# Second shifted copy in two halves, each on VectorE or GpSimd, in a newly planned order

## The chip, the cores and the metric

The kernel runs on one core of a Trainium2 chip. The time is device microseconds (us) of one execution. Three executions of the kernel before took 707.72, 704.95 and 707.62 us, so its median is 707.62 us.

## The reference, cut to what matters

Two attention blocks read the same input x (2048 tokens, 512 features, 32 heads of 16), and a gate per token mixes them. Block B is the expensive one: full softmax attention, 32 heads of 2048 x 2048 scores.

```python
def _A_ref(x, wqkv, w_phi, wo):
    ...
    pq = jnp.einsum("bhsd,hdf->bhsf", q, w_phi)
    pk = jnp.einsum("bhsd,hdf->bhsf", k, w_phi)
    phi_q = jnp.concatenate([_softmax(pq, axis=-1), _softmax(-pq, axis=-1)], axis=-1)
    phi_k = jnp.concatenate([_softmax(pk, axis=-1), _softmax(-pk, axis=-1)], axis=-1)
    kv = jnp.einsum("bhsf,bhsd->bhfd", phi_k, v)
    ...
    num = jnp.einsum("bhqf,bhfd->bhqd", phi_q, kv)
    den = jnp.einsum("bhqf,bhf->bhq", phi_q, z)[..., None] + 1e-6
    ...

def _B_ref(x, wqkv, wo):
    ...
    scores = jnp.einsum("bhqd,bhkd->bhqk", q, k) * (Dh ** -0.5)
    p = _softmax(scores, axis=-1)
    o = jnp.einsum("bhqk,bhkd->bhqd", p, v)
    return (lambda x, *d: x.transpose(*d))(o, 0, 2, 1, 3).reshape(B, S, D) @ wo

x = A_x
g = _sigmoid((x * gate_w).sum(-1, keepdims=True))
a = _A_ref(x, A_wqkv, A_w_phi, A_wo)
b = _B_ref(x, B_wqkv, B_wo)
return g * a + (1 - g) * b
```

## The kernel before, in words

**Sets and tiles of block B.** The work of block B is cut into 32 sets (`N_SETS`): four chunks of 512 queries, in each four groups of eight heads, in each two sets of four heads. A set runs over 16 key tiles of 128 keys. For one key tile TensorE multiplies keys by queries for four heads: four score products (`qk`, line 1231), each 128 x 512 into one bank of the PSUM tensor `psR`, which has seven banks. The exponential of the scores comes from one of two engines:

- ScalarE takes two banks at a time and writes a tile `E` (line 1246, a 128 x 1024 exponential), so two instructions make a key tile. There are 12 buffers for `E`.
- VectorE makes a cheap exponential: it scales a bank of scores into the bits of a bfloat16 number and writes them as int16 into a tile `T` (line 1251, 128 x 512, four instructions for a key tile). To make this exact enough, two shifted copies of `T` are made, `TS` = `T` + 43 and `TS` = `T` + 85 in integers. The products with the values then use three weighted terms. The first copy is always VectorE's (line 1263, one instruction over 128 x 2048). The second (`m >= PSH`) is either the same on VectorE or, on GpSimd, an addition of int32 numbers that hold two int16 each (line 1266, 128 x 1024 int32).

Then TensorE multiplies with the values (`pv`, line 1282, four matmuls of 18 columns side by side) into the one bank `psO`: one round for an `E` key tile, three rounds for a `T` key tile. At the end of a set VectorE copies `psO` into `OT` (line 866), a transposing DMA and two VectorE instructions (lines 1172, 1174) normalise it, and the next set's first `pv` has to wait for that copy of `psO`.

**The rest.** In the first sets also run: the projections of keys, queries and values of all groups (lines 883 and 945, evacuated mostly by VectorE), the gate (line 988: 64 matmuls with one column each, in four parts; then an exponential on ScalarE, line 992, and `omg`, lines 993 to 995), the product of block A's projection with `w_phi` (line 1006, 128 x 128 matmuls, evacuated by VectorE into `Wp`) and a check of magnitudes (sums of squares by matmuls with `ones`, line 1023, maxima on VectorE into `ct`). From set 4 on block A runs in between: projections, exponentials on ScalarE (line 1074), sums and normalisation on GpSimd (lines 1080 to 1090), from set 13 on also the second half of block A (`nums`, line 1150) and the output products (line 1326).

**What sets the order.** Nothing of the order is written by hand. When the kernel is built, a list scheduler (`_Sched`) places every operation with a planned cost (`occ`), a priority and the buffers that are free, and issues the operations of each engine in that planned order. Waits on semaphores are derived from the plan. Whether a key tile goes to ScalarE or VectorE, and whether the second copy goes to VectorE or GpSimd, is chosen in the plan too: both forms are offered as alternatives (`alt`), and the first that the plan can place wins (`choose`). The tuple `STYLES` holds one number for every 3 us of the plan. It seeds the thresholds by which the scheduler weighs score products against other work in that stretch, so another tuple is another order.

The plan keeps VectorE's copies (`kind="sh"`) and GpSimd's work apart in time: a GpSimd operation gets a dependency on the latest VectorE copy planned before it, and a VectorE copy is planned behind the GpSimd work that has been placed (`port`, in `_earliest` and `advance`).

After planning, `fill` looks for stretches of 3.413 us in which the planned work of TensorE is under a share (`CELLS`) of full use of its array, and puts idle matmuls (products with zeros into `psO`, line 1379) into gaps there. In that sum a gate part counts 0 and `nums` counts 1.

Of the kernel before, what the change touches and what calls it, by code (L numbers as in the profile page):

```python
# [38 lines left out]
GT = 2.2  # L39
# [27 lines left out]
Q32, PSH, SHP = 1, 2, 1.88  # L67
# [5 lines left out]
HAM, CELLS = 3.413, 0.46  # L73
# [35 lines left out]
class _Sched:  # L109
# [58 lines left out]
    def _place(self, o, at):  # L168
# [21 lines left out]
        for slots, ts in single.items():  # L190
            times = self._slot_times(slots)
            if len(times) < len(ts):
                return None, None
            got = sorted(times, key=lambda i: (max(times[i], when), -i))[:len(ts)]
            when = max([when] + [times[i] for i in got])
            where += list(zip(ts, sorted(got)))
# [191 lines left out]
    def fill(self, make, narrow, last_pv, set_O):  # L388
# [10 lines left out]
        for i, o in enumerate(pe):  # L399
# [3 lines left out]
                0.0 if o.name in ("gate", "gsum") else 1.0)  # L403
# [310 lines left out]
def _build(ctx, nc, A_x, A_wqkv, A_w_phi, A_wo, B_wqkv, B_wo, gate_w, out):  # L714
# [76 lines left out]
    def st_(x):  # L791
        return T0 + P_SET * x
# [190 lines left out]
    for part in range(4):  # L983
# [7 lines left out]
        gops.append(add("pe", st_(GT), 0.9, gate_mm, deps=sum(op_x, []) + op_gw, tiles=[tg], mode="full", name="gate", nb=st_(GT - 0.7)))  # L991
# [211 lines left out]
    for s in range(N_SETS):  # L1203
# [12 lines left out]
        for eng, frac, kt in todo:  # L1216
# [40 lines left out]
            else:  # L1257
                di = DSET.index(kt)
                sh = []
                for m, X in ((1, T1), (2, T2)):  # L1260
                    two = m >= PSH
                    a2 = lambda eng: alt + ((("sh", s, kt, m), eng),) if two else alt
                    sh.append([add("dve", pr + 1.0 + 0.3 * m, 0.6, lambda e, T=T, X=X, m=m: e.tensor_single_scalar(  # L1263
                        X.ap, T.ap, SHIFT[m], ALU.add), deps=exps, tiles=[T, X], name="sh", kind="sh", alt=a2("dve"))])
                    if two:
                        sh[-1].append(pool(pr + 1.0 + 0.3 * m, SHP, lambda e, T=T, X=X, m=m: e.tensor_tensor(  # L1266
# [194 lines left out]
```

## Time and profile before

| | |
|---|---|
| median of three runs | 707.62 us (704.95 to 707.72) |
| profiled execution, its own time | 709.42 us |
| its span (first to last instruction) | 707.6 us |
| mean granted TensorE clock | 0.99 of full speed |
| exponentials on ScalarE (line 1246) | 692, i.e. 346 key tiles |
| scaled scores on VectorE (line 1251) | 664, i.e. 166 key tiles |
| copies on VectorE (line 1263) | 205: 166 first and 39 second ones |
| second copies on GpSimd (line 1266) | 127 |

The span is 1.8 us shorter than the time of the same execution. Busy time is the time in which an engine had at least one instruction running. Consecutive instructions of ScalarE or VectorE overlap at their ends, so a run of n instructions takes less than n times the mean of one. The lines of the profile stand in the prediction, where they are used.

### The profile page before, as it was taken

How to read it: one execution, taken by the hardware profiler on the slowest of the kernel's cores; microseconds unless marked ns; L12 is line 12 of the kernel's file. 1: busy time of each engine (PE TensorE's matmuls, PEld its weight loads, DVE VectorE, ACT ScalarE, POOL GpSimd, SP SyncE). 2: the span in 40 equal slices, each digit the busy share in tenths (PEclk: the TensorE clock that was granted, in tenths of full speed). 3: DMA queues.
4: the chain of work that ended last, by engine and by line, in shares of the span. 5: the costliest groups of instructions: out<-in, count | busy, mean ns of one | idle time of the engine just before them, and what ended most of it. 6: DMA issues, size and time to landing. Idle time of an engine off the chain costs nothing.

```text
span 707.6 us, 16129 instructions
## 1 busy us (share of the span) xinstructions
PE 657.1 (93%) x6632; PEld 208.6 (29%) x6632; DVE 667.4 (94%) x1191; ACT 679.7 (96%) x769; POOL 429.3 (61%) x364
## 2 busy tenths in 40 slices
PE   8999999999999999989999999999999999988895
PEld 3333343332322222222222322222222222222222
DVE  5998899999999999999999999999999999999995
ACT  6999799999999999999999999999999999999994
POOL 5468666655756656656667766666666755566541
PEclk9999899999999999999999999999999999999998
DMA  6501000011000000102111121112212111220001
GB/s 145 154 16 10 13 12 16 17 59 25 10 16 16 9 17 8 24 8 36 34 31 38 46 54 28 40 40 45 38 31 47 42 32 35 38 45 9 16 9 34
DMA packets 72192, 23.80 MB, mean 34 GB/s; under 512 B 64048, under 2 KB 72112, under 8 KB 72112
## 3 DMA queue, kind: packets, MB, share of 16 engines
q1 hardware_dynamic: 70896, 21.93, 14.7%
q8 instruction: 53, 0.87, 0.6%
q10 hardware_dynamic: 1216, 0.79, 0.4%
q14 instruction: 27, 0.22, 0.1%
HBM read 4.21 MB, written 2.10 MB: 9 GB/s over the span
## 4 chain that ended last, share of the span: by engine, by line
ACT 77%; PE 15%; DVE 5%; DMA 1%; issue 0%
ACT E L1246 73%; PE psR L1231 5%; PE psO L1282 4%; PE psR L883 3%; DVE T L1251 3%; ACT phk L1074 2%; ACT WAT L1074 2%; PE psR L1326 1%; PE psR L945 1%; DMA OTT<-OT 1%; DVE TS L1263 1%; PE psR L897 1%; PE psR L1023 0%; DVE vB L950 0%; PE psR L1006 0%
## 5 line engine op out<-in xcount | busy, mean ns | idle before, releaser
L1246 ACT ACTIVATE E<-psR 128x1024 bf16<-128x1024 f32 x692 | 649.1, 1118 | 12.0 <-PE psR L1231 10.9
L1251 DVE TENSOR_SCALAR T<-psR 128x512 int16<-128x512 f32 x664 | 424.1, 678 | 19.9 <-PE psR L1231 16.5
L1231 PE MATMUL psR<-qz,kT 32*128 32x512 bf16 (+1 forms) x2048 | 294.0, 386 | 39.9 <-ACT E L1246 27.9
L1266 POOL TENSOR_TENSOR TS<-T,shc 128x1024 int32<-128x1024 int32 x127 | 240.4, 1893 | 94.9 <-DVE TS L1263 78.1
L1231 PEld LDWEIGHTS psR<-qz,kT 32*128 32x128 bf16 (+1 forms) x2048 | 77.6, 91 | 292.3 <-ACT E L1246 212.7
L1263 DVE TENSOR_SCALAR TS<-T 128x2048 int16<-128x2048 int16 x205 | 137.0, 683 | 0.4
L1282 PE MATMUL psO<-E,vB 128*18 128x512 bf16 x1384 | 126.1, 385 | 0.1
L1282 PE MATMUL psO<-TS,vS 128*18 128x512 bf16 x1328 | 122.1, 384 | 0.0
L1282 PE MATMUL psO<-T,vB 128*18 128x512 bf16 x664 | 65.6, 386 | 0.0
L1090 POOL TENSOR_TENSOR phk<-phk,ss 128x1024 bf16<-128x1024 bf16 x16 | 30.9, 1929 | 31.9 <-DVE TS L1263 31.9
L1085 POOL TENSOR_TENSOR tr<-WAT 128x256 f32<-128x256 f32 x32 | 23.3, 729 | 37.8 <-DVE TS L1263 37.8
L1090 POOL TENSOR_TENSOR WAT<-WAT,ss 128x1024 bf16<-128x1024 bf16 x16 | 30.9, 1929 | 25.2 <-DVE TS L1263 25.2
L1282 PEld LDWEIGHTS psO<-TS,vS 128*18 128x18 bf16 x1328 | 29.9, 88 | 54.8 <-issue 38.2
L1282 PEld LDWEIGHTS psO<-E,vB 128*18 128x18 bf16 x1384 | 31.6, 88 | 44.4 <-issue 31.0
L883 PE MATMUL psR<-xT,WB 128*128 128x512 bf16 x128 | 33.2, 383 | 0.4 <-ACT WAT L1074 0.3
L883 PE MATMUL psR<-Wp,xT 128*128 128x512 bf16 x128 | 33.2, 382 | 0.0
L1080 POOL TENSOR_TENSOR WAT<-WAT 128x512 f32<-128x512 bf16 x16 | 18.5, 1155 | 21.2 <-DVE TS L1263 16.3
L1282 PEld LDWEIGHTS psO<-T,vB 128*18 128x18 bf16 x664 | 16.2, 88 | 20.9 <-issue 17.0
L866 DVE CAST OT<-psO 128x512 bf16<-128x512 f32 x31 | 21.1, 682 | 0.1
L958 POOL TENSOR_SCALAR vS<-vB 128x144 bf16<-128x144 bf16 (+1 forms) x32 | 11.9, 373 | 14.4 <-DVE TS L1263 12.2
L1080 POOL TENSOR_TENSOR WAT<-phk 128x512 f32<-128x512 bf16 x16 | 18.5, 1156 | 2.9 <-DVE TS L1263 2.3
L1086 POOL TENSOR_TENSOR tr<-tr 128x128 f32<-128x128 f32 x32 | 12.8, 400 | 11.0 <-DVE TS L1263 9.4
(114 smaller groups left out, 412.2 us busy)
## 6 DMA issues: line engine op xcount, KB each, us to landing
qz<-qst SPq DMA_DIRECT2D x120, 16.0 KB, 1.8
out_dram<-WAv SPq DMA_DIRECT2D x12, 128.0 KB, 1.7
WB<-in_B_wqkv_dram SPq DMA_DIRECT2D x3, 384.0 KB, 5.3
T<-in_A_x_dram SPq DMA_DIRECT2D x2, 256.0 KB, 4.4
T<-in_A_x_dram ACTq DMA_DIRECT2D x2, 256.0 KB, 4.7
WAv<-in_A_wqkv_dram SPq DMA_DIRECT2D x1, 512.0 KB, 6.6
WB<-in_A_wo_dram SPq DMA_DIRECT2D x1, 512.0 KB, 3.4
WB<-in_B_wo_dram SPq DMA_DIRECT2D x1, 512.0 KB, 3.6
```

The lines of the kernel that those rows point to most:

```text
L866: return add("dve", prio, 0.6, lambda e: e.tensor_copy(dst(), src()), deps=deps, tiles=tiles, name=name)
L883: calls = [lambda e, t=t: e.matmul(tile.ap[:, off:off + 512], lhsT=lhs(t), rhs=rhs(t), start=(t == 0), stop=(t == KT - 1)) for t in range(KT)]
L1074: ex = [add("act", prio, 0.48, lambda e, s=s: e.activation(ev()[:, :, 16 * s:16 * s + 16], P(), ACTF.Exp, scale=1.0 - 2.0 * s), deps=[f] + ...
L1080: p1 = pool(prio + 2, 1.23, lambda e: e.tensor_tensor(v8(), eg()[:, :, 0:8], eg()[:, :, 8:16], ALU.add), ex + use_wat, tiles=[ee, tr], nam ...
L1085: p2 = pool(prio + 2, 0.92, lambda e: e.tensor_tensor(u4(), v8()[:, :, 0:4], v8()[:, :, 4:8], ALU.add), [p1], tiles=[tr, tr2])
L1090: return pool(prio + 6, 1.95, lambda e: e.tensor_tensor(eg(), eg(), ss.ap[:, 1, :].unsqueeze(2).to_broadcast([128, 64, DH]), ALU.mult), [o ...
L1231: ins = e.matmul(rs[h].ap, lhsT=kT[a:a + n, g, 128 * kt:128 * (kt + 1)], rhs=qt.ap[a:a + n, c, :], start=True, stop=True, tile_position=(a ...
L1246: exps.append(add("act", pr + 0.5 * cc, 0.905, lambda e, rs=rs, E=E: e.activation(E.ap.rearrange("p (a n) -> p a n", n=512), pair(rs), ACT ...
L1251: exps.append(add("dve", pr + 0.5 * cc + 0.01 * h, 0.6, lambda e, rs=rs, T=T, cc=cc, h=h: e.tensor_scalar(T.ap[:, 1024 * cc + 512 * h:1024 ...
L1263: sh.append([add("dve", pr + 1.0 + 0.3 * m, 0.6, lambda e, T=T, X=X, m=m: e.tensor_single_scalar(X.ap, T.ap, SHIFT[m], ALU.add), deps=exps ...
L1266: sh[-1].append(pool(pr + 1.0 + 0.3 * m, SHP, lambda e, T=T, X=X, m=m: e.tensor_tensor(X.ap.bitcast(I32), T.ap.bitcast(I32), shc[:, m - 1: ...
L1282: ins = e.matmul(O.ap[32 * col:32 * col + VW, :], lhsT=lhs(hd), rhs=rhs(cc)[:, 512 * h:512 * (h + 1)], start=(first_pv[s] == key), stop=(l ...
```

## The change

The second copy of a VectorE key tile is split into two halves of 1024 columns. Each half depends only on the two banks of scores that it copies (before: on all four), and each half goes by itself to VectorE (128 x 1024 int16, planned at 0.33 us) or to GpSimd (128 x 512 int32, planned at 1.0 us, before 1.88 us for the whole). `fill` weighs gate parts with 0.03 (before 0) and `nums` with 0.5 (before 1), and its bound `CELLS` goes from 0.46 to 0.48. The four gate parts get priorities 4.2 us apart. Among equally early buffers the scheduler now prefers one whose neighbours are not free. `STYLES` has new numbers throughout.

```diff
-    0, 0, 0, 151809, 629345, 652452, 168322, 738033, 102229, 862790, 0, 980301, 810598, 366361, 0, 572306, 687424, 829696, 0,
...
+    0, 0, 0, 0, 542087, 842781, 403435, 999872, 741538, 35173, 144778, 419920, 885871, 0, 0, 738596, 364495, 542020, 977492, 0,
...
-Q32, PSH, SHP = 1, 2, 1.88
+Q32, PSH, SHP = 1, 2, 1.0
...
-HAM, CELLS = 3.413, 0.46
+CLOSE = 0.0
+HAM, CELLS = 3.413, 0.48
...
-            got = sorted(times, key=lambda i: (max(times[i], when), -i))[:len(ts)]
+            at = {i: max(t, when) for i, t in times.items()}
+            got = sorted(times, key=lambda i: (at[i], sum(times.get(j, 1e9) <= at[i] + CLOSE for j in (i - 1, i + 1)), -i))[:len(ts)]
...
-                0.0 if o.name in ("gate", "gsum") else 1.0)
+                {"gate": 0.03, "gsum": 0.03, "nums": 0.5}.get(o.name, 1.0))
...
-        gops.append(add("pe", st_(GT), 0.9, gate_mm, deps=sum(op_x, []) + op_gw, tiles=[tg], mode="full", name="gate", nb=st_(GT - 0.7)))
+        gops.append(add("pe", st_(GT + 0.2 * part), 0.9, gate_mm, deps=sum(op_x, []) + op_gw, tiles=[tg], mode="full", name="gate", nb=st_(GT - 0.7 + 0.2 * part)))
...
-                    a2 = lambda eng: alt + ((("sh", s, kt, m), eng),) if two else alt
-                    sh.append([add("dve", pr + 1.0 + 0.3 * m, 0.6, lambda e, T=T, X=X, m=m: e.tensor_single_scalar(
-                        X.ap, T.ap, SHIFT[m], ALU.add), deps=exps, tiles=[T, X], name="sh", kind="sh", alt=a2("dve"))])
-                    if two:
-                        sh[-1].append(pool(pr + 1.0 + 0.3 * m, SHP, lambda e, T=T, X=X, m=m: e.tensor_tensor(
-                            X.ap.bitcast(I32), T.ap.bitcast(I32), shc[:, m - 1:m].to_broadcast([128, 1024]), ALU.add),
-                            exps + op_shc, "shp", [T, X], a2("pool")))
+                    parts = [(0, 1024), (1024, 2048)] if two else [(0, 2048)]
+                    sh.append([])
+                    for lo, hi in parts:
+                        a2 = lambda eng: alt + ((("sh", s, kt, m, lo), eng),) if two else alt
+                        sh[-1].append(add("dve", pr + 1.0 + 0.3 * m, 0.33 if two else 0.6, lambda e, T=T, X=X, m=m, lo=lo, hi=hi: e.tensor_single_scalar(
+                            X.ap[:, lo:hi], T.ap[:, lo:hi], SHIFT[m], ALU.add), deps=exps[lo // 512:hi // 512], tiles=[T, X], name="sh", kind="sh", alt=a2("dve")))
+                        if two:
+                            sh[-1].append(pool(pr + 1.0 + 0.3 * m, SHP, lambda e, T=T, X=X, m=m, lo=lo, hi=hi: e.tensor_tensor(
+                                X.ap[:, lo:hi].bitcast(I32), T.ap[:, lo:hi].bitcast(I32), shc[:, m - 1:m].to_broadcast([128, 512]), ALU.add),
+                                exps[lo // 512:hi // 512] + op_shc, "shp", [T, X], a2("pool")))
```

Both programs can be built and their instructions listed in order, without times. All counts that differ:

| engine, instruction | before | after |
|---|---|---|
| ScalarE exponential `E`, 128 x 1024 | 692 | 696 |
| VectorE scaled scores `T`, 128 x 512 | 664 | 656 |
| VectorE copy `TS`, 128 x 2048 | 205 | 164 (the first copies) |
| VectorE copy `TS`, 128 x 1024 | 0 | 90 |
| GpSimd copy `TS`, 128 x 1024 int32 | 127 | 0 |
| GpSimd copy `TS`, 128 x 512 int32 | 0 | 238 |
| TensorE `pv` matmuls from `E` / `T` / `TS` | 1384 / 664 / 1328 | 1392 / 656 / 1312 |
| TensorE idle matmuls | 68 | 92 |

Two key tiles move from VectorE to ScalarE. Of the 328 half copies of the 164 VectorE key tiles, VectorE makes 90 and GpSimd 238.

The order around the gate on TensorE, after (the changed kernel's lines are one or a few higher: 989 gate, 1007 `Wbd`, 1024 `ones`, 884 projections, 1232 score products, 1286 `pv`):

```
L1024 psR<-phk,ones x2
L989  psR<-gw,xT 128x1 x16        (gate part)
L1051 psR<-gw,ones x4
L1007 psR<-Wbd,WAT 128x128 x4
L1232 psR<-qz,kT x4               (score products)
L989  psR<-gw,xT 128x1 x16        (gate part)
L1007 psR<-Wbd,WAT 128x128 x4
L989  psR<-gw,xT 128x1 x16        (gate part)
L1007 psR<-Wbd,WAT 128x128 x4
L1024 psR<-phk,ones x2
L989  psR<-gw,xT 128x1 x16        (gate part)
L1024 psR<-phk,ones x2
L1232 psR<-qz,kT x1               (one score product)
L1007 psR<-Wbd,WAT 128x128 x4
L884  psR<-xT,WB x4
L1007 psR<-Wbd,WAT 128x128 x4
L884  psR<-xT,WB x4
L1286 psO<-TS x8, E x4, T x4, TS x8, E x16   (ten groups of four)
L1232 psR<-qz,kT x4               (score products)
```

VectorE's order there, after: `Wp` x3, one maximum into `ct`, `T` x1, `omg`, `Wp`, `omg`, whole copies x3, `OT`. The first `E` group of the `pv` run above waits for VectorE, behind the last two `TS` groups of the set. In the order before, the four gate parts stand between score products: 16 gate matmuls, 6 score products, 32, 6, 16, then 4 + 8 small ones, 4 score products, seven groups of `pv`, 4 score products.

25 rows, old and new, of the table STYLES are left out of this document.

## The prediction

> **What bounds the kernel now.** I read the busy times, the chain of work that ended last, the waits, and then the busy time by stage.
>
> ```profile
> PE 657.1 (93%) x6632; PEld 208.6 (29%) x6632; DVE 667.4 (94%) x1191; ACT 679.7 (96%) x769; POOL 429.3 (61%) x364
> ...
> ACT 77%; PE 15%; DVE 5%; DMA 1%; issue 0%
> ```
>
> Three engines are nearly full, ScalarE (ACT) most, and 77% of the last chain is ScalarE. The stages show where it isn't full (first the stretch, then for each engine busy us and instructions, at the end granted clock and DMA):
>
> ```profile
> core 0: us, PE busy (x) PEld busy (x) DVE busy (x) ACT busy (x) POOL busy (x), PEclk, DMA share, GB/s
> 0.00:10.00 10.00, 8.61 (x50) 4.56 (x52) 3.08 (x9) 3.92 (x6) 7.36 (x29) 1.00 0.59 146
> 10.00:40.00 30.00, 27.69 (x293) 11.18 (x289) 28.98 (x50) 29.87 (x34) 13.43 (x14) 1.00 0.55 131
> 40.00:70.00 30.00, 29.11 (x318) 10.95 (x315) 26.63 (x46) 27.89 (x31) 21.57 (x19) 1.00 0.10 13
> 70.00:80.00 10.00, 9.52 (x116) 4.34 (x116) 8.04 (x15) 6.85 (x9) 7.58 (x5) 0.66 0.07 15
> 80.00:110.00 30.00, 29.57 (x324) 11.96 (x323) 28.21 (x48) 28.17 (x31) 19.01 (x16) 1.00 0.05 10
> 110.00:150.00 40.00, 38.95 (x386) 13.48 (x378) 39.60 (x76) 38.93 (x46) 25.08 (x24) 1.00 0.06 15
> 150.00:350.00 200.00, 186.24 (x1904) 56.52 (x1904) 194.53 (x342) 198.99 (x232) 122.18 (x113) 1.00 0.10 22
> 350.00:360.00 10.00, 9.31 (x80) 2.10 (x78) 8.13 (x17) 8.93 (x12) 5.52 (x6) 0.83 0.18 34
> 360.00:690.00 330.00, 307.66 (x3098) 89.65 (x3097) 321.19 (x579) 328.39 (x369) 205.66 (x144) 1.00 0.17 35
> 690.00:707.60 17.60, 10.45 (x91) 3.82 (x88) 8.99 (x18) 7.73 (x10) 1.89 (x1) 0.87 0.11 34
> ```
>
> ScalarE's idle time is stretch less busy: 6.1 us at the start and 9.9 at the end, and between them 0.1 + 2.1 + 3.2 + 1.8 + 1.1 + 1.0 + 1.1 + 1.6 = 12.0 us. Of these, 7.1 lie in 40 to 110, where TensorE and VectorE also carry projections, gate and checks. 4.2 lie in two ten-us stretches with a granted clock of 0.66 and 0.83. From 150 on ScalarE is idle 3.7 us in 540. So the span is ScalarE's work plus 16.0 us at the ends plus 12.0 us of starving, and the change can win only from those 12.0. Who starves it:
>
> ```profile
> ACT E L1246 <- PE psR L1231: 10.9, 25, 1.7
> DVE T L1251 <- PE psR L1231: 16.5, 41, 1.2
> POOL TS L1266 <- DVE TS L1263: 78.1, 53, 5.3
> PEld psO L1282 <- DVE TS L1263: 4.6, 19, 0.5
> PEld psO L1282 <- POOL TS L1266: 3.0, 11, 0.4
> ```
>
> (Total us, times, longest.) ScalarE waits only for score products that TensorE makes late. The copies, which are what is changed, hold TensorE for 7.6 us in 30 waits, and GpSimd's long waits behind VectorE's copies cost nothing by themselves.
>
> **The change, part by part.**
>
> ```profile
> 604.90 59.81 ACT L1246 ACTIVATE E<-psR 128x1024 bf16<-128x1024 f32 x65
> 599.99 3.68 DVE L1251 TENSOR_SCALAR T<-psR 128x512 int16<-128x512 f32 x6
> 22.03 1.28 DVE L1263 TENSOR_SCALAR TS<-T 128x2048 int16<-128x2048 int16 x2
> 9.46 1.13 DVE L939 TENSOR_SCALAR qz<-qst,qmask 128x512 bf16<-128x512 bf16 x4
> ...
> L1246 ACT ACTIVATE E<-psR 128x1024 bf16<-128x1024 f32 x692 | 649.1, 1118 | 12.0 <-PE psR L1231 10.9
> L1251 DVE TENSOR_SCALAR T<-psR 128x512 int16<-128x512 f32 x664 | 424.1, 678 | 19.9 <-PE psR L1231 16.5
> L1266 POOL TENSOR_TENSOR TS<-T,shc 128x1024 int32<-128x1024 int32 x127 | 240.4, 1893 | 94.9 <-DVE TS L1263 78.1 <-PE psO L1282 6.5 <-PE psR L1231 4.7
> L1263 DVE TENSOR_SCALAR TS<-T 128x2048 int16<-128x2048 int16 x205 | 137.0, 683 | 0.4
> L1080 POOL TENSOR_TENSOR WAT<-WAT 128x512 f32<-128x512 bf16 x16 | 18.5, 1155 | 21.2 <-DVE TS L1263 16.3 <-DVE ob L1174 5.0
> ```
>
> *ScalarE.* 65 exponentials in a row take 59.81 us and the last lasts 1.12, so one follows another after 58.69 / 64 = 0.917 us. Four more are 3.7 us on the bounding engine, with no cover: **+3.7**.
>
> *VectorE.* In a row, `T` costs (3.68 - 0.68) / 5 = 0.60 us and a whole copy 1.28 - 0.68 = 0.60. Gone are 8 `T`, 2 first and 39 second copies: 49 x 0.60 = 29.4 us. New are 90 half copies, which no row shows. Half of 0.60 is the lower bound (27.0 us in all), a whole 0.60 the upper (54.0). The nearest shorter row, 512 columns, costs (1.13 - 0.35) / 3 = 0.26, and the straight line from there to 0.60 at 2048 columns gives 0.37 at 1024, which I take: 33.3. VectorE gets 3.9 us more (-2.4 to +24.6). From 10 to 690 the stages leave it 24.7 us idle, 16.5 of it in `T` waiting for scores, and that hides 3.9: 0 on the path. Uncovered it would be those 3.9.
>
> [...]
>
> *GpSimd.* 127 x 1.893 = 240.4 us go, 238 half copies come. Half of 1.893 is 0.95 and the 512-column addition of line 1080 takes 1.155, so 225 to 275, and I take 1.02, nearer the half because the operation is the same: 243. GpSimd is idle 278 us of the span, which hides it. But VectorE's copies, each of which holds back the GpSimd work planned behind it, rise from 205 to 254, and all copy instructions from 332 to 492. If TensorE's 7.6 us of waits on copies grew alike, by 1.48, TensorE would lose 3.7 us. It is idle 50 us, and ScalarE feels only what delays scores: I take **+0.5** (from -1, since a half is ready sooner, to +3.7).
>
> *TensorE.* Six more groups of idle matmuls and four fewer `pv` groups, 0.22 us each (the distance of two such groups in the rows below), are +0.4 us in gaps: 0. Uncovered it is 0.4.
>
> *The order.* The place that I can price is the gate. Rows for the stretch before:
>
> ```profile
> 65.19 8.36 ACT L1246 ACTIVATE E<-psR 128x1024 bf16<-128x1024 f32 x9
> 73.40 0.23 ACT L992 ACTIVATE ez<-psR 128x16 f32<-128x16 f32 x1
> 75.28 2.01 ACT L1246 ACTIVATE E<-psR 128x1024 bf16<-128x1024 f32 x2 [1.65 <-PE psR L1231]
> 78.78 1.94 ACT L1246 ACTIVATE E<-psR 128x1024 bf16<-128x1024 f32 x2 [1.49 <-PE psR L1231]
> ...
> 70.26 0.95 PE L988 MATMUL psR<-gw,xT 128*128 128x1 bf16 x32
> 79.34 0.39 PE L1006 MATMUL psR<-Wbd,WAT 128*128 128x128 bf16 x4
> 79.56 0.59 PE L1023 MATMUL psR<-phk,ones 128*128 128x512 bf16 x2
> 357.72 1.04 PE L883 MATMUL psR<-Wp,xT 128*128 128x512 bf16 x4
> 356.78 0.39 PE L1282 MATMUL psO<-TS,vS 128*18 128x512 bf16 x4
> 357.00 0.39 PE L1282 MATMUL psO<-E,vB 128*18 128x512 bf16 x4
> ...
> 74.31 0.69 DVE L866 CAST Wp<-psR 128x512 bf16<-128x512 f32 x1
> ```
>
> Rows show about 0.17 us of tail behind the last matmul, so back to back 16 gate matmuls cost about 0.4 us, four small ones 0.22, two `ones` 0.42, a projection 0.87, a `pv` group 0.22. In the order after, between four score products (two pairs for ScalarE) and the next four stand three gate parts, four blocks of small ones, two of `ones`, one score product, two projections and ten `pv` groups: 1.2 + 0.9 + 0.8 + 0.1 + 1.7 + 2.2 = 6.9 us in which ScalarE gets nothing new. Two pairs, with at most one already running, feed it 1.8 to 2.7 us, so it starves at least 4.2 us. VectorE makes it longer: the `pv` run can't pass the set's end until VectorE has done four `Wp`, a maximum, a `T`, three whole copies and `OT`, ten times about 0.6 us, partly from before the stretch; then eight `pv` groups (1.7 us) follow before new scores. That is 7.7 us after its first `Wp`, and 1.5 to 2 later since it has to wait for what it evacuates: up to 7.5 us of starving, more if the clock falls as it did here. I take 6.5, against 3.2 in 70 to 80 before: **+3.3**. In return some of the work that starved ScalarE in 40 to 70 and 80 to 110 (3.9 us) is now in that burst: between -3.9 and 0, I take half, **-2.0**.
>
> *The clock.* More idle matmuls and the lower weight of `nums` may keep the clock up at the place of 350 to 360, worth 1.1 at most: **-0.5**. [...]
>
> *The rest* (0.1 + 1.1 + 1.0 + 1.6 = 3.8 us of starving): with nothing to tell them apart 0, between -2 and +6. *The ends*: the last copies are a half, a whole and a half where two wholes stood, at most +0.2: 0.
>
> Sum: 3.7 + 0.5 + 3.3 - 2.0 - 0.5 = +5.0 us. The span of 707.6 becomes 712.6 and the profiled execution's 709.42 becomes 714.4. That execution is 1.8 us above the median of the runs, so against the median the forecast is 707.6 + 5.0 = **712.6 us**, 0.7% slower.
>
> **The rivals.** *The plan takes the starving away (faster).* Half copies wait for two banks, not four, and fit into shorter holes, so scores are never late. The floor, with no idle time but the ends, is 707.6 + 3.7 - 12.0 = 699.3. If the 12.0 falls to 3.5, the time is 702.8. For it: 7.1 of the 12.0 lie in one planned region, 4.2 beside a low clock. Against it: the burst above alone asks for over 4.2. It decides when the middle starves less than 4.8 us in all.
>
> [...]
>
> *The burst replaces the region (no change).* If all of 40 to 110 shrinks to the burst (7.1 to 6.5) and the second low clock and 2 us of the rest go, the time is 707.6 + 3.7 - 0.6 - 1.1 - 2.0 = 707.6.
>
> *VectorE becomes the bound (slower still).* If a half copy costs 0.5 us, VectorE gets 15.6 us more and its 24.7 us of idle time goes down to 9. At the margin the two engines then share the work badly, and about half of the 15.6 shows: 715 to 720. For it: VectorE is 94% busy. Against it: the 512-column row at 0.26.
>
> That the split doesn't happen is no rival: the built order has 90 and 238 halves.
>
> **How the numbers follow.** The forecast has 0.45 (its own range, by the bounds of burst, region and copy waits, is 710 to 717), the faster rival 0.29, no change 0.17, VectorE as the bound 0.09. A measurement of this kernel can tell about 0.5% from no change, so faster means below 704.1 us and slower above 711.2. A small part of the forecast's range lies below 711.2, about 0.05 of its 0.45. So faster 0.29, same 0.22, slower 0.49. The range of 702 to 718 leaves out the best of the faster rival (about 0.12) and the worst of the VectorE one (0.06).
>
> **What would show it.** ScalarE's busy time should rise from 679.7 to about 683.4. One stretch before 110 us should show it idle for 5 us or more within ten, with gate parts on TensorE. The copy lines should read about 0.4 us more often on VectorE and about 1.0 us on GpSimd, with TensorE's waits on copies near 11 us. The prediction is wrong if ScalarE's idle time between the first and last exponential falls below 8, or if VectorE's idle time is eaten up.

## The result, and the profile after

| | before | after |
|---|---|---|
| median of 8 executions, us | 708.08 (704.95 to 710.95) | 713.32 (711.60 to 715.03) |
| ratio to before | | 1.0078, 95% interval 1.0057 to 1.0100 |
| profiled execution, us | 709.42 | 712.39 |
| its span, us | 707.6 | 710.6 |
| its granted clock | 0.990 | 0.998 |

The changed kernel is 0.8% slower. The two profiled executions are only 3.0 us apart, because that of before lies 1.3 us above its median and that of after 0.9 below; what can be shown row by row is therefore 3.0 of the 5.2 us.

From the page of the changed kernel, the busy times and the engines of the chain that ended last (64 matmul records are missing from this profile, 6576 against 6640 weight loads, so TensorE's busy time reads too low in all its rows):

```profile
PE 646.1 (91%) x6576; PEld 206.3 (29%) x6640; DVE 666.4 (94%) x1232; ACT 681.7 (96%) x773; POOL 432.2 (61%) x475
...
ACT 79%; PE 14%; DVE 4%; POOL 1%; issue 1%; POOLq 0%; DVEq 0%
```

Busy time by stage in the changed kernel, with the columns of the prediction's table (TensorE, its weight loads, VectorE, ScalarE, GpSimd, granted clock, DMA share, GB/s):

```profile
0.00:10.00 10.00, 7.98 (x52) 3.74 (x52) 3.95 (x12) 4.69 (x7) 7.46 (x29) 1.00 0.61 146
10.00:40.00 30.00, 28.46 (x296) 11.78 (x304) 29.33 (x52) 29.20 (x34) 15.74 (x18) 1.00 0.55 133
40.00:70.00 30.00, 28.25 (x327) 12.22 (x325) 20.43 (x36) 24.39 (x28) 26.87 (x25) 1.00 0.03 6
70.00:80.00 10.00, 8.25 (x97) 2.61 (x94) 9.33 (x20) 6.37 (x7) 5.42 (x4) 1.00 0.10 25
80.00:110.00 30.00, 28.32 (x304) 10.68 (x300) 29.61 (x52) 29.54 (x33) 17.74 (x20) 1.00 0.05 11
110.00:150.00 40.00, 37.81 (x388) 13.18 (x395) 38.71 (x75) 39.32 (x45) 25.48 (x32) 1.00 0.08 15
150.00:350.00 200.00, 182.04 (x1883) 56.85 (x1901) 193.89 (x359) 199.00 (x234) 125.47 (x136) 1.00 0.09 21
350.00:360.00 10.00, 8.85 (x95) 2.32 (x93) 9.62 (x22) 10.00 (x13) 4.52 (x6) 1.00 0.27 56
360.00:690.00 330.00, 303.36 (x3039) 88.53 (x3059) 319.65 (x589) 328.31 (x370) 200.29 (x206) 1.00 0.17 35
690.00:710.60 20.60, 12.75 (x130) 4.42 (x127) 11.83 (x26) 10.85 (x13) 3.17 (x4) 0.91 0.09 29
```

Both low clocks are gone: 70 to 80 and 350 to 360 have 1.00, where before had 0.66 and 0.83. ScalarE's idle time (stretch less busy) is 5.3 us at the start, 9.75 at the end, and 0.8 + 5.6 + 3.6 + 0.5 + 0.7 + 1.0 + 0 + 1.7 = 13.9 in the middle, against 12.0 before. The 3.0 us of the spans follow: 2.0 more of busy time (681.7 less 679.7), 1.9 more of idle time in the middle, 0.9 less at the two ends. Between 40 and 110 us ScalarE is idle 9.7 us (before 7.1).

The groups of that profile, VectorE's copies kept apart by size (busy us, mean ns, idle time before them):

```profile
L1247 ACT ACTIVATE E<-psR 128x1024 bf16<-128x1024 f32 x696 | 650.9, 1131 | 10.1 <-PE psO L1286 5.4 <-PE psR L1232 3.5
L1270 POOL TENSOR_TENSOR TS<-T,shc 128x512 int32<-128x512 int32 x238 | 243.8, 1039 | 104.6 <-DVE TS L1267 83.6 <-DVE ob L1175 7.0 <-PE psO L1286 4.4
L1267 DVE TENSOR_SCALAR TS<-T 128x2048 int16<-128x2048 int16 x164 | 111.6, 686 | 0.2
L1267 DVE TENSOR_SCALAR TS<-T 128x1024 int16<-128x1024 int16 x90 | 35.5, 417 | 0.2 <-PE psO L1286 0.2
```

The waits of the same profile (total us, times, longest):

```profile
DVE T L1252 <- PE psR L1232: 13.5, 34, 1.1
PEld psO L1286 <- DVE TS L1267: 7.2, 28, 0.4
ACT E L1247 <- PE psO L1286: 5.4, 1, 5.4
PEld psO L1286 <- POOL TS L1270: 3.6, 15, 0.4
ACT E L1247 <- PE psR L1232: 3.5, 15, 0.5
```

Before, ScalarE waited 10.9 us in 25 short waits for scores. Now 5.4 of its idle time is a single wait, for a `pv` group (line 1286) that has to free an `E` buffer. The order in time around it, for ScalarE, TensorE and VectorE in turn (start, us, what, and in brackets the idle time before it):

```profile
54.49 10.25 ACT L1247 ACTIVATE E<-psR 128x1024 bf16<-128x1024 f32 x11
68.03 0.18 ACT L993 ACTIVATE ez<-psR 128x16 f32<-128x16 f32 x1 [3.28 <-PE psR L989]
73.63 6.56 ACT L1247 ACTIVATE E<-psR 128x1024 bf16<-128x1024 f32 x7 [5.42 <-PE psO L1286]
...
71.65 0.73 PE L1286 MATMUL psO<-TS,vS 128*18 128x512 bf16 x8
73.18 0.39 PE L1286 MATMUL psO<-E,vB 128*18 128x512 bf16 x4 [0.81 <-DVE OT L867]
...
70.71 1.82 DVE L1267 TENSOR_SCALAR TS<-T 128x2048 int16<-128x2048 int16 x3
72.45 0.68 DVE L867 CAST OT<-psO 128x512 bf16<-128x512 f32 x1
```

ScalarE stops at 64.74, does the small gate exponential, and goes on at 73.63: 3.28 + 5.42 = 8.7 us of starving. The first 3.28 us it waits for the gate itself, since the gate's exponential stands next in its order. TensorE spends the stretch on gate, checks and projections. The next set's `pv` stand behind them in its order, and wait until the last set is out of `psO`, behind three whole copies that VectorE does from 70.71 on; that wait is 0.81 us of TensorE's time.

### The profile page after: what moved, and what is told of

Read it like the earlier page. It is cut to its first block, busy times and chain, and to the rows that moved or that the text cites. A ratio compares the mean times of both kernels' runs of the same rounds, so it can differ in the third digit from the quotient of the medians.

```text
span 710.6 us, 16239 instructions
## 1 busy us (share of the span) xinstructions
PE 646.1 (91%) x6576; PEld 206.3 (29%) x6640; DVE 666.4 (94%) x1232; ACT 681.7 (96%) x773; POOL 432.2 (61%) x475
## 4 chain that ended last, share of the span: by engine, by line
ACT 79%; PE 14%; DVE 4%; POOL 1%; issue 1%; POOLq 0%; DVEq 0%
ACT E L1247 74%; PE psR L1232 5%; PE psO L1286 4%; ACT WAT L1075 2%; ACT phk L1075 2%; DVE T L1252 2%; PE psR L884 2%; PE psR L1330 2%; PE psR L946 2%; DVE TS L1267 1%; PE psR L1024 1%; DVE OT L867 0%; POOL qz L845 0%; DVE Wp L867 0%; ACT Wp L1349 0%
## 5 line engine op out<-in xcount | busy, mean ns | idle before, releaser
L1252 DVE TENSOR_SCALAR T<-psR 128x512 int16<-128x512 f32 x656 | 419.2, 679 | 16.7 <-PE psR L1232 13.5
L1270 POOL TENSOR_TENSOR TS<-T,shc 128x512 int32<-128x512 int32 x238 | 243.8, 1039 | 104.6 <-DVE TS L1267 83.6
L1267 DVE TENSOR_SCALAR TS<-T 128x2048 int16<-128x2048 int16 (+1 forms) x254 | 142.7, 591 | 0.4 <-PE psO L1286 0.2
L1286 PE MATMUL psO<-TS,vS 128*18 128x512 bf16 x1312 | 120.3, 382 | 0.2
L884 PE MATMUL psR<-xT,WB 128*128 128x512 bf16 x111 | 29.5, 381 | 4.0 <-issue 1.9
L884 PE MATMUL psR<-Wp,xT 128*128 128x512 bf16 x103 | 27.5, 380 | 4.9 <-issue 2.4
L1075 ACT ACTIVATE WAT<-psR 128x512 bf16<-128x512 f32 x32 | 19.0, 704 | 0.5 <-PE psR L884 0.5
L1075 ACT ACTIVATE phk<-psR 128x512 bf16<-128x512 f32 x32 | 19.3, 719 | 0.0
```

The source lines that it names most:

```text
L884: calls = [lambda e, t=t: e.matmul(tile.ap[:, off:off + 512], lhsT=lhs(t), rhs=rhs(t), start=(t == 0), stop=(t == KT - 1)) for t in range(KT)]
L1075: ex = [add("act", prio, 0.48, lambda e, s=s: e.activation(ev()[:, :, 16 * s:16 * s + 16], P(), ACTF.Exp, scale=1.0 - 2.0 * s), deps=[f] + ...
L1252: exps.append(add("dve", pr + 0.5 * cc + 0.01 * h, 0.6, lambda e, rs=rs, T=T, cc=cc, h=h: e.tensor_scalar(T.ap[:, 1024 * cc + 512 * h:1024 ...
L1267: sh[-1].append(add("dve", pr + 1.0 + 0.3 * m, 0.33 if two else 0.6, lambda e, T=T, X=X, m=m, lo=lo, hi=hi: e.tensor_single_scalar(X.ap[:, ...
L1286: ins = e.matmul(O.ap[32 * col:32 * col + VW, :], lhsT=lhs(hd), rhs=rhs(cc)[:, 512 * h:512 * (h + 1)], start=(first_pv[s] == key), stop=(l ...
```

## The experiments

Every time below is compared with executions of the kernel before that were taken beside it (medians 707.6 to 708.5 us). Where a ratio is turned into us it is (ratio - 1) x 708. The ratios are those on record and not quotients of the medians; the two differ most for the kernel without idle matmuls (1.0121 and 714.94 / 708.46 = 1.0091). Code is shortened to what matters.

**First theory: the 8.7 us of starving at the gate are the cost.** Four kernels took the change apart.

*The kernel before, each second copy issued as two halves in place.*

```diff
-  e.tensor_single_scalar(X.ap, T.ap, SHIFT[m], ALU.add)
+  [e.tensor_single_scalar(X.ap[:, lo:hi], T.ap[:, lo:hi], SHIFT[m], ALU.add)
+   for lo, hi in ([(0, 1024), (1024, 2048)] if m >= PSH else [(0, 2048)])][-1]
```

(and GpSimd's form alike)

> The kernel before in its own planned order; only each second copy (39 on VectorE, 127 on GpSimd) is issued as two half copies one directly behind the other, where the one whole copy stood. Theory (the newly planned order costs the time, not the half copies): GpSimd pays about 2 x 1.0 - 1.89 = 0.1 us more for each copy and VectorE about 2 x 0.33 - 0.60 = 0.1, all of it beside ScalarE: 707 to 710 us, ratio 0.999 to 1.003. Rival (the half copies cost the time themselves): most of the +5.2 us is here, ratio 1.005 or more.

Measured: 709.22 us (12 executions), ratio 1.0021, interval 1.0009 to 1.0032, so +1.5 us (0.6 to 2.3). Two rows of its order in time, and the waits of TensorE (its weight loads) on copies:

```profile
295.45 0.75 DVE L1264 TENSOR_SCALAR TS<-T 128x1024 int16<-128x1024 int16 x2
...
159.38 2.03 POOL L1267 TENSOR_TENSOR TS<-T,shc 128x512 int32<-128x512 int32 x2
```

```profile
PEld psO L1284 <- POOL TS L1267: 6.8, 23, 0.5
PEld psO L1284 <- DVE TS L1264: 6.6, 27, 0.5
```

Two halves in a row take 0.75 us on VectorE, the second 0.75 - 0.42 = 0.33 us behind the first, and 2.03 on GpSimd, where the whole took 1.89. TensorE's waits on copies rise from 7.6 to 13.4 us. So halving alone costs about a quarter of the loss: the theory stands here. Even that may not all be the halves: these executions had a mean clock of 0.991 where those of before beside them had 0.993, an estimated 0.9 us by the line given with the four added kernels below.

*The changed kernel with the starving relieved.* After its order is planned, two copies, the eviction of the set's result, seven `pv` groups, three pairs of score products and the exponentials that they feed are moved forward; the numbers are positions in the order that the operations are written in (the four moves of exponentials on ScalarE are not shown).

```diff
+    move("dve", (1173, 1189), 1188, 56.5)               # two whole copies
+    move("pe", (1179, 1195), 1245, 63.95)               # their pv groups
+    move("dve", (1213,), 371, 65.55)                    # OT
+    move("pe", (1222, 1227, 1232, 1237, 1242), 1250, 66.27)   # the next set's pv from E
+    move("pe", (1253,), 330, 68.62); move("pe", (1255,), 374, 69.35); move("pe", (1258,), 375, 70.60)
```

> The changed kernel; after its order is planned, around 64 to 74 us two whole copies and the eviction of the set's result are moved forward on VectorE, and seven matmul groups of that set's end and the next one's start and three pairs of score products forward on TensorE, between the gate's parts. Nothing else moves. Theory (ScalarE's 8.7 us of idle time around 64.75 to 73.63 is the cost): that idle time falls to about 4, the time falls by 3 to 5 us against the changed kernel: 708 to 710 us, ratio 1.000 to 1.004. Rival (TensorE and VectorE, which do the same work as before the edit, give it back later): 712 us or more, ratio 1.006 or more, and ScalarE's idle time behind 110 us grows from 3.1 to 6 or more.

Measured: 713.31 us, ratio 1.0075 (1.0054 to 1.0095), the same as without the edit. Two stretches of before, of after and of this kernel:

```profile
40.00:110.00 70.00, 68.21 (x755) 27.24 (x752) 62.89 (x108) 62.92 (x69) 48.16 (x38) 0.95 0.08 12
110.00:690.00 580.00, 542.16 (x5459) 161.75 (x5451) 563.46 (x1011) 575.25 (x655) 358.45 (x284) 1.00 0.14 29
```

```profile
40.00:110.00 70.00, 64.83 (x718) 25.52 (x719) 59.37 (x105) 60.31 (x67) 50.03 (x48) 1.00 0.05 11
110.00:690.00 580.00, 532.06 (x5395) 160.88 (x5442) 561.88 (x1042) 576.64 (x657) 355.75 (x378) 1.00 0.14 29
```

```profile
40.00:110.00 70.00, 67.63 (x731) 25.76 (x728) 60.07 (x105) 60.81 (x67) 51.41 (x48) 1.00 0.05 11
110.00:690.00 580.00, 540.53 (x5445) 160.74 (x5437) 561.83 (x1042) 576.72 (x657) 354.85 (x378) 1.00 0.15 29
```

Neither account was right. The five exponentials were done inside the gap, but ScalarE then waited 5.14 us for the next scores at 78 us: its idle time in 40 to 110 went only from 9.7 to 9.2, and behind 110 it stayed at 3.3 (3.4 without the edit), so nothing was given back later either. TensorE does the same gate, check and projection work whichever exponentials are served in between. This reordering moved the starving and didn't remove it, so the run doesn't say what the 8.7 us cost; a count of exponentials below does.

*Only the two copies moved forward* (the first line of the edit above).

> The changed kernel with only two of the three late whole copies moved forward on VectorE, from about 71 us to about 56 us; TensorE's order stays. Theory (the late copies cost because TensorE's order was planned around them, not by a wait in the execution): TensorE can save at most its 0.81 us wait on the eviction of the set's result: 712 to 713.5 us, ratio 1.005 to 1.008. Rival (the wait on the copies itself holds TensorE): the time falls as in burst_relieved, ratio 1.003 or less.

Measured: 716.65 us, ratio 1.0108 (1.0086 to 1.0131): slower than both expected, by 2.1 us over the changed kernel by the ratios. Its profile lost the clock at the gate, and a projection there (line 884) that takes 1.04 us elsewhere took 1.92. Stretches of one us around it, clock in the third column from the end:

```profile
65.00:66.00 1.00, 1.00 (x25) 0.76 (x22) 0.66 (x1) 0.00 (x0) 1.00 (x2) 0.96 0.00 0
66.00:67.00 1.00, 1.00 (x23) 0.80 (x22) 0.69 (x1) 0.00 (x0) 1.00 (x2) 0.50 0.00 0
...
72.00:73.00 1.00, 1.00 (x8) 0.61 (x6) 0.00 (x0) 0.00 (x0) 0.96 (x1) 0.62 0.00 0
73.00:74.00 1.00, 1.00 (x11) 0.15 (x9) 0.00 (x0) 0.00 (x0) 0.08 (x1) 1.00 0.00 0
```

It says nothing of the copies, since the clock covers it; it shows what the gate's stretch can cost.

*The kernel before with the new weights for idle matmuls.*

```diff
-                0.0 if o.name in ("gate", "gsum") else 1.0)
+                {"gate": 0.03, "gsum": 0.03, "nums": 0.5}.get(o.name, 1.0))
-HAM, CELLS = 3.413, 0.46
+HAM, CELLS = 3.413, 0.48
```

> The kernel before in its own planned order, with the changed kernel's weights for thin matmuls and its share of 0.48: 20 groups of idle matmuls in place of 17, the added ones where projections for output and query end a thin stretch. Theory: the granted clock in 350 to 360 us rises from 0.83 to about 1 and ScalarE gets back up to 1.1 us there: 706.5 to 708.5 us, ratio 0.998 to 1.0005. Rival (idle matmuls take time from the scores): three groups of 0.22 us, ratio 1.001 or more.

Measured: 707.96 us, ratio 1.0006 (0.9991 to 1.0022). No cost and no gain that can be told apart. The low clock behind 350 us is gone in its profile (350 to 450 has 1.00 where before had 0.98), but 10 to 40 has 0.94.

**Second theory: TensorE sets the pace up to about 150 us and ScalarE from there, so the four more exponentials are the cost.** It came from the relieved kernel, and from the count of exponentials: up to 150 us the profiles of before and after show 135 each. Four kernels add work of one engine at one place, to the kernel before in its own order: an exponential done once more into a spare tile, or a projection done twice.

```diff
+    for o in exps[i] ...:              # late: i = 200, 320, 440, 560; early: 44, 58, 72, 86
+        e.activation(scratch, pair(rs), ACTF.Exp, scale=SCALE)
+    for o in sch.order["pe"]:          # late: qf01, qf11, qf21, qf31; early: kf12, vf12, kf13, vf13
+        o.fn = lambda e, fn=o.fn: (fn(e), fn(e))[1]
```

> The kernel before in its own order, with four more exponentials of 128x1024 on ScalarE (the 201st, 321st, 441st and 561st are first done once into a tile that nobody reads), all behind 200 us. New theory (TensorE sets the pace up to about 150 us, ScalarE from there on, so that the changed kernel's four more exponentials are its cost): 4 x 0.917 = 3.7 us, 711 to 712.5 us, ratio 1.004 to 1.0065. Rival (three engines share the pace, and a late exponential is half hidden): 709 to 710.5 us, ratio 1.0015 to 1.0035.

> The same four more exponentials, but between about 55 and 105 us (the 45th, 59th, 73rd and 87th). New theory (TensorE sets the pace there): 0 to 1.2 us, ratio 1.000 to 1.002, and ScalarE's idle time in 40 to 110 falls by 2.5 to 3.7. Rival (ScalarE sets the pace there too, and its idle time is only that of the gate): 3 to 4 us, ratio 1.004 or more.

> The kernel before in its own order, with four projections on TensorE between about 50 and 62 us (keys and values of two token blocks) done twice in place, where ScalarE is not starved yet: 4 x about 0.87 = 3.5 us more of TensorE. New theory (TensorE sets the pace up to about 150 us): 2 to 3.7 us, ratio 1.003 to 1.005. Rival (only the gate's stretch starves ScalarE, whatever TensorE has to do elsewhere): within 1 us, ratio 0.999 to 1.0015.

> The kernel before in its own order, with four projections of queries between about 165 and 290 us done twice in place: the same 3.5 us more of TensorE. New theory (ScalarE sets the pace from about 150 us on): 0 to 1 us, ratio 0.999 to 1.0015. Rival (TensorE is as near to the bound there as early on): 2 us or more, ratio 1.003 or more.

| added to before | us of work | median, us | ratio (95% interval) | us |
|---|---|---|---|---|
| four exponentials behind 200 us | 3.7 | 711.65 | 1.0062 (1.0044 to 1.0080) | +4.4 |
| four exponentials in 55 to 105 | 3.7 | 713.13 | 1.0068 (1.0047 to 1.0089) | +4.8 |
| four projections in 50 to 62 | 3.5 | 711.04 | 1.0051 (1.0036 to 1.0066) | +3.6 |
| four projections in 165 to 290 | 3.5 | 712.92 | 1.0074 (1.0054 to 1.0095) | +5.2 |

The theory falls in its stages: an early exponential and a late projection show in full too (with the early exponentials ScalarE's idle time in 40 to 110 was 6.4 us against 7.1, where the theory asked for 2.5 to 3.7 less), and TensorE's idle time of about 14 us between 150 and 350 hides nothing. In the kernel with the late projections, ScalarE's stretch is

```profile
150.00:350.00 200.00, 186.55 (x1889) 57.04 (x1889) 191.69 (x336) 195.95 (x228) 120.36 (x111) 1.00 0.09 22
```

4.05 us idle, where before had 1.0: behind each of the four doubled projections ScalarE waits 0.5 to 0.8 us for scores, so the scores that stand ready in the banks don't bridge it. (The two kernels with the largest losses also had the lowest mean clock, 0.990 against 0.993; over 34 executions of before a straight line gives 0.39 us for each 0.001 of clock, so some 1.3 us of each are the clock.)

**Third theory: the planned order has no room, in any engine and in either direction.**

*Ten more half copies on VectorE, in the kernel before.*

```diff
+    e.tensor_single_scalar(scratch, T.ap[:, 0:1024], SHIFT[m], ALU.add)     # ahead of 10 whole copies
```

> The kernel before in its own order, with ten more half copies of 1024 columns on VectorE, into a tile that nobody reads, each directly before a whole copy between about 217 and 570 us. By the rows of the changed kernel a half in a row takes about 0.33 us: 3.3 us more of VectorE. Theory (the planned order leaves no engine room, so that added work shows wherever it stands): 710.5 to 711.5 us, ratio 1.004 to 1.006. Rival (VectorE's idle time of 16 us in that stretch hides it, as the prediction has it for 3.9 us): 707 to 708.7 us, ratio 0.999 to 1.0015.

Measured: 710.35 us, ratio 1.0031 (1.0014 to 1.0048), +2.2 us (1.0 to 3.4): between the two, about two thirds of the 3.3 us show. The mean clock was 0.991 where before had 0.992, so by the same line an estimated 0.5 us of it is the clock.

*The changed kernel with less of ScalarE's work.*

```diff
+    brief.update({o.key: 64 for o in [o for o in sch.order["act"] if o.kind == "exp"][150:640:65]})
...
-  E.ap.rearrange("p (a n) -> p a n", n=512), pair(rs)
+  E.ap.rearrange("p (a n) -> p a n", n=512)[:, :, 0:n], pair(rs)[:, :, 0:n]     # n = 64 for eight, else 512
```

> The changed kernel in its own order, with eight of its 696 exponentials (the 151st and every 65th behind it) done for 128 of their 1024 columns; the rest of those eight tiles is left out. Each should take about 0.2 us in place of 0.917, so ScalarE has about 5.6 us less. Theory (what ScalarE has to do is the time, in both directions): 707 to 709 us, ratio 0.999 to 1.002 against the kernel before. Rival (work added shows in full because each engine waits for the next, but work taken away from one engine alone is held back by the other two): 711 us or more, ratio 1.0045 or more.

Measured: 712.62 us, ratio 1.0065 (1.0045 to 1.0086). From its page:

```profile
PE 657.7 (93%) x6640; PEld 207.6 (29%) x6640; DVE 665.9 (94%) x1232; ACT 676.9 (95%) x773; POOL 431.4 (61%) x475
```

ScalarE has 4.8 us less to do than in the changed kernel and the time falls by 0.0013 of 708, 0.9 us, which is within the intervals. Most of the rest became idle time: 18.2 us in the middle against 13.9 (1.2 of the rise in 10 to 40, where this profile's clock was 0.94). The two traces show what the shortening itself gave. The 146th exponential, ahead of the first short one, starts 1.72 us later than in the changed kernel's trace (163.95 against 162.23), the 651st only 0.02 later (656.59 against 656.57): about 1.7 of the 4.8 us came back. So the time is as the rival has it: of work taken from ScalarE alone only about a third comes back, while work added to it showed in full. The theory's "either direction" falls.

*The changed kernel without idle matmuls* (`CELLS` 0.48 becomes 0).

> The changed kernel without any of its 23 groups of idle matmuls: 23 x 0.22 = 5.1 us less of TensorE. Theory (they stand in planned gaps and cost nothing, and hold the clock up): the granted clock falls below 0.995 and the time is 713.5 us or more, ratio 1.0075 or more. Rival (on TensorE too every group shows): the time falls by 3 to 5 us, ratio 1.003 or less.

Measured: 714.94 us, ratio 1.0121 (1.0086 to 1.0156), clock 0.992 in the profile. 5.1 us less of TensorE made it no faster. Its executions had a mean clock of 0.988 where the changed kernel's had 0.997, an estimated 3.5 us by the line above, so what the groups cost by themselves this run can't show. Where its profile lost the clock:

```profile
310.00:320.00 10.00, 9.04 (x101) 3.54 (x98) 8.97 (x18) 9.42 (x12) 5.12 (x5) 0.83 0.07 16
...
330.00:340.00 10.00, 9.78 (x98) 2.81 (x96) 8.42 (x18) 9.31 (x12) 5.60 (x6) 0.88 0.23 47
```

ScalarE starves 1.3 us in these two stretches. In the changed kernel both have a clock of 1.00 and no idle time.

**The fourth corner: the new order with whole copies.** After planning, the first of two halves on one engine is dropped and the second does the whole copy.

```diff
+    for a, b in (x for x in found.values() if len(x) == 2):
+        b.fn = b.unit                       # the whole copy
+        b.deps += [d for d in a.deps if d not in b.deps]
+        sch.order[a.eng].remove(a)
...
```

> The changed kernel in its own order, with whole second copies again: where both halves of a copy stand on the same engine (31 pairs on VectorE, 105 on GpSimd) the first is left out and the second does all 2048 columns; 28 copies whose halves stand on different engines stay as they are. With split_in_place it makes the fourth corner of old and new order by whole and half copies. Theory (the halves cost what they did in the old order, about 1.5 us, and the new order the rest, about 3.7): 711 to 712.5 us, ratio 1.004 to 1.0065. Rival A (the halves are the cost in this order): 708 to 709.5 us, ratio 1.002 or less. Rival B (in this order the earlier half is what feeds TensorE, so that whole copies come too late): 714.5 us or more, ratio 1.009 or more.

Measured: 718.56 us, ratio 1.0146 (1.0121 to 1.0170): rival B. TensorE waits more on copies. Its weight loads wait 17.2 us in the first two rows, where the changed kernel had 10.8 (7.2 and 3.6), and the matmuls themselves wait 5.3 us on GpSimd's copies in the third, where all of the changed kernel's `TS` matmuls have 0.2 us of idle time before them:

```profile
PEld psO L1291 <- POOL TS L1276: 11.1, 19, 1.3
PEld psO L1291 <- DVE TS L1267: 6.1, 20, 0.9
PE psO L1291 <- POOL TS L1276: 5.3, 8, 1.0
```

| ratio to before | whole copies | half copies |
|---|---|---|
| old order | 1 | 1.0021 |
| new order | 1.0146 (28 of 164 copies still halved) | 1.0078 |

Read across, halves cost 0.2% in the order that was planned for whole copies and gain 0.7% (4.8 us) in the order that was planned for halves. Read down, the new order costs 0.6% (4.0 us) with halves in both. Each ratio is known to about 0.2%, so the gain and the cost of the order are clear of that, the cost of the halves barely, and the sizes are rough. So it is the newly planned order, with its four more exponentials, that loses, and there the halves make it lose less. How much is not shown: in this corner a whole copy stands where its second half stood, later than a planner would have put it, so part of its 1.0146 is that placing.

None of these kernels beats the kernel before.

## Why the prediction came out right, point by point

The forecast of +5.0 us held, and the loss sits, as its sum had it, in what the new order does and not in the half copies. That the sum came so close is in part luck: counted by busy and idle time the exponentials' term came out 1.7 us lower, the gate's region 1.3 higher and the clock 0.6 better, and 2.2 us of the medians are in no row. Several terms stand for something else than the prediction said.

- *Four more exponentials, +3.7.* The price is right: four more cost the old order 4.4 us (3.1 to 5.7). The reason is only half right: "on the bounding engine, with no cover" would have them come back when taken away, and eight shorter ones in the new order gave back about 1.7 of 4.8 us in the trace and 0.9 in the time. ScalarE is busiest, but TensorE and VectorE keep step with it. Its busy time rose by 2.0 and not 3.7, to 681.7 where 683.4 was forecast.
- *VectorE, +3.9 hidden: 0.* The half was sized 0.37 and is 0.33 in a row; VectorE ended 1.0 us below before (666.4), so there was nothing to hide. The step "from 10 to 690 the stages leave it 24.7 us idle, and that hides 3.9" was wrong as a step: of 3.3 us added to the kernel before, 2.2 showed (1.0 to 3.4).
- *GpSimd and the waits on copies, +0.5.* Halves 1.039 us (taken 1.02), 243.8 us in all (243), TensorE's waits 10.8 us (11). But these are waits of its weight loads, and the prediction read them as "hold TensorE for 7.6 us": the `TS` matmuls themselves have 0.0 us of idle time before them in before and 0.2 here, by ends that the profile models. In the old order 5.8 us more of such waits went with +1.5 us, a quarter; a quarter of the 3.2 here would be 0.8, an estimate that nothing tests.
- *Idle matmuls, 0.* Right within 0.15%: the new weights alone gave 1.0006 (0.9991 to 1.0022).
- *The burst at the gate, +3.3.* It came at 64.7 to 73.6, with the gate parts, and was 8.7 us, beyond the 7.5 that the prediction called the most unless the clock fell, and it didn't fall. What was missed: not the scores held ScalarE but first the gate (3.28 us) and then a full `E` buffer (5.42), whose `pv` stood late in TensorE's order; VectorE's late copies are at most 0.81 of it. As a lasting cost it is not borne out: the 60th exponential starts 6.7 us later than in before (76.37 against 69.71), the 200th, with the same other ScalarE work behind it, 1.0 later (217.00 against 216.03), and by 640 us it is level, as the rows below show.
- *The rest of 40 to 110, -2.0.* It became 9.7 - 8.7 = 1.0, from 3.9: -2.9. Both together are +2.6 (forecast +1.3).
- *The clock at 350 to 360, -0.5.* It was -1.1, the bound: the clock there is 1.00, before 0.83. That more idle matmuls keep it up was the author's estimate, and the runs show this much of it: the new weights in the old order had 1.00 in 350 to 450 (before 0.98) but 0.94 in 10 to 40 (before 1.00), and the new order without idle matmuls had 0.83 and 0.88 in 310 to 320 and 330 to 340, where with them it had 1.00.
- *The rest and the ends.* +0.4 and -0.9, where 0 was taken.

With measured sizes the terms are 2.0 + 2.6 - 1.1 + 0.4 - 0.9 = 3.0, the difference of the two spans. The other 2.2 us of the medians lie between executions without a profile, and no row shows them. About 1.2 of them may be the clock, an estimate by the line of 0.39 us for each 0.001: the profiled execution of before had 0.990, its executions beside the experiments 0.993 on average.

The 3.0 us can also be counted by exponentials. This is the last run of them, in before and in after:

```profile
639.70 56.39 ACT L1246 ACTIVATE E<-psR 128x1024 bf16<-128x1024 f32 x61
639.28 59.93 ACT L1247 ACTIVATE E<-psR 128x1024 bf16<-128x1024 f32 x65
```

In both kernels 631 exponentials and the same other work of ScalarE lie behind it. The changed kernel begins it 0.42 us earlier, although it starved more (0.33 us later than the kernel before with the new weights, whose clock held at 350 us), and then does four more: 3.54 us. By this count the loss in the profiles is the prediction's first term, and the stall at the gate was made up but for 0.3 us at most. It shows where the time stands and not what the new order would cost with 692 exponentials, which no run has.

Open is which decision of the new plan costs the 4.0 us: the two key tiles that move to ScalarE, the shorter price for GpSimd's copy, the new rule for banks, the gate's priorities and the halves all act on one sequential plan, and each undone gives another order altogether. No such plan was run.

Of the rivals, *the plan takes the starving away* would have needed less than 4.8 us of ScalarE's idle time in the middle; it was 13.9. *The burst replaces the region* would have needed 40 to 110 to fall to 6.5; it rose to 9.7. *VectorE becomes the bound* would have needed a half at 0.5 us.

## What to carry to other kernels

In a schedule planned as tightly as this one over three nearly full engines with few buffers between them, idle time of an engine is poor cover: price a microsecond added at about one on ScalarE (here 4.4 and 4.8 us for 3.7 added) and TensorE (3.6 and 5.2 for 3.5), the largest two with an estimated 1.3 of clock in them, and at half or more on VectorE (2.2 for 3.3), and expect only a part back from a microsecond taken from one engine alone (0.9 us for 4.8 taken from ScalarE). When an edit makes a planner decide anew, separate the two by running the edit in the old order and the old form in the new order; here the edit cost 0.2% and the order 0.6%. A long stall in one place is not yet a cost: count behind it how far each kernel has come before it is blamed.

## What was not expected of the hardware

**A busy TensorE that loses its clock.** In the kernel with two copies moved, TensorE is busy 0.84, 1.00, 0.69 and 1.00 of each us from 62 to 66, by ends that the profile models and in part with gate matmuls of one column, and its clock falls to 0.50 there. The changed kernel has the same four shares in the same four us and keeps 1.00, so the busy share alone doesn't decide it. From the clock shares the half clock lasts from 65.92 to 72.76, 6.84 us. In before, at the same work:

```profile
71.00:72.00 1.00, 0.79 (x14) 0.35 (x11) 0.68 (x2) 1.00 (x2) 1.00 (x1) 0.82 0.00 0
72.00:73.00 1.00, 1.00 (x15) 0.30 (x12) 0.19 (x1) 1.00 (x2) 1.00 (x2) 0.50 0.00 0
...
78.00:79.00 1.00, 1.00 (x13) 0.44 (x10) 0.82 (x2) 0.22 (x1) 0.10 (x1) 0.77 0.22 46
```

0.82 puts its start at 71.64 and 0.77 its end at 78.46: 6.82 us again. The dip behind 350 us in before, 0.83 over ten us, is about half as long: it reads 0.77 in 351 to 352, 0.50 in the next two us and 0.53 in 354 to 355, so by the same count it lasts from 351.54 to 354.94, 3.40 us. Whether the edit of the two VectorE copies decided it here is not shown.

**The time of one kernel follows its clock.** The 34 executions of before beside the first eight experiments run from 704.41 us at 0.996 to 710.52 at 0.988. The changed kernel's eight lie at 0.995 to 0.999, better than before, and are slower all the same.
